# A fused attention and feed-forward kernel: the written-out instruction order of its head is replaced, and the products without a result stand elsewhere

## The chip, the cores and the metric

The kernel runs on one core of a Trainium2 chip. The metric is the device time of one execution in microseconds (us); the time of a version is the median of several runs. Before the change it is 657.39 us, the median of 3 runs (656.91 to 659.03).

## What is computed

```python
# q, k, v: (4 batches, 8 heads, 768 positions, 64); float32
k_sum = k.reshape(B, H, 24, 32, D).max(axis=3)      # a summary key per 32 positions
v_sum = v.reshape(B, H, 24, 32, D).mean(axis=3)     # a summary value per 32 positions
scores_l = scale * q @ k.T          # only |i - j| < 16 is kept, the rest gets -1e9
scores_s = scale * q @ k_sum.T + log(32)
a = softmax(concatenate([scores_l, scores_s]))
attn = a @ concatenate([v, v_sum])
x = attn with heads side by side    # (3072 tokens, 512)
out = ((x @ w_a) * (x @ w_b)) @ w_out               # d_ff = 1536
```

The result has to agree with a float32 computation, so each float32 operand of the large products is split into a high part that TensorE takes in one pass (fp32r) and the rest, a low part.

## The kernel before

**Tiles.** A tile is 128 query positions with all heads. Tokens are worked in chunks: batch 0 in three chunks of two tiles, batches 1 to 3 in chunks of three tiles. For a chunk the attention is computed first, then 12 items of the feed-forward part: item f takes the columns f*128 and on of `w_a` and `w_b` (line 1121: two accumulations h), multiplies the two (DVE), splits the product into gh and gl (ACT, DVE) and multiplies by a row block of `w_out` (line 1243: accumulation into the banks o0 to o3).

**The head.** Until the first item can start, the first four tiles of batch 0 go through a special path, `first_attention`. It has these steps, which the prediction speaks of:

- six loads of keys (line 353, 256 KB each), each turned by four transposes on TensorE (line 503), copied to `kT` by ACT (561, 562), and reduced to block maxima by DVE (569);
- four loads of queries (256 KB each), also turned by line 503 and scaled by ACT (978);
- the mask product (691) and the scores (704), both into the banks o0 to o3; maxima on DVE (737), 32 exponentials a pair of tiles on ACT (751), reciprocals (760, 771) and a diagonal matrix (778) on DVE; a product that turns and normalizes the weights at once (799), its copy by ACT (811);
- the block means of v: six loads ("halves of v", 256 KB each, tiles space10 to space12 of the queue's rows below), an addition of neighbours on POOL (1005), a product with a 0 to 1/32 matrix (996) into bank h0, copies by ACT (1014) and POOL (1020) into the value tiles vw0, vw1 and space12;
- the loads of the value rows of a tile (three loads of 64 to 192 KB), the product of weights and values (852), and its split into x (ACT 881, DVE 885), from which the first item reads.

Beside this, the weights are converted to high and low parts: a load (385, 512 KB) brings half a pair, ACT extracts (420), DVE shifts, masks and multiplies (428, 435, 441), ACT rounds (473), POOL forms the low part (478, 484). Weights are converted in this way until about 150 us.

**What sets the order.** Every operation is recorded with `add` (class `Work`, line 107) and gets a number. `emit` (132) then writes the instructions engine by engine. Without a table it plans with costs in numbers; for the head, `ORDER` (line 24) is a table that for each of the five engines lists the numbers of the operations one after the other. An operation is written only when it is the next one of its engine's list; when a list has run out, the planner goes on by its own rules. SP issues almost all DMAs, also in the order of its list. An engine runs its instructions strictly in the written order, so one that waits holds all behind it.

**Products without a result.** `SPIN` (line 97) lists 16 products of the identity by itself, with the bank that they write and their width (line 1354). Nothing reads them. They are recorded last, as operations 2676 to 2691, and only the list of TensorE says where they stand:

```python
for bk, n in SPIN:
    pe(-1, n / 600, (), (), lambda bk=bk, n=n: nc.tensor.matmul(bank[bk][:, :n], ident, ...))
```

Of the kernel before, what the change touches and what calls it, by code (L numbers as in the profile page):

```python
# [25 lines left out]
        2676 2677 13 2678 5 2679 1 2680 2681 21 2682 17 9 2683 75 57 55 77 58 78 2684-2686 96 98  # L26
        2687-2689 111 100 113 121 102 141 123 104 106 124 143 151 2690 153 154 2691 115 145 173
        171 542 543 180 175 550 178 548 182 549 555 557 556 558 565 563 564 572 570 573 571 582
        583 580 578 581 579 588 590 354 591-593 602 589 600 598 603 599 601 612 610 611 613 608
        609 622 618 623 620 619 621 632 630 628 633 629 631 642 643 640 638 641 639 650 648 510  # L30
        652 673 653 649 651 662 660 658 661 682 659 667 679 687 668 688 940 941 948 946 947 793
        955 953 954 962 960 849 961 967-969 976 974 975 983 903 981 829 982 990 997 988 989 1004
        995 996 883 1002 1003 1046 1009 1011 1018 1010 937 1016 1017 1023 1024
    """,
    "ACT": """
# [8 lines left out]
        806 809 958 802 963 965 970 972 857 977 855 854 862-864 861 865 979 856 689 984 858 986  # L44
        830 991 993 998 915 917 918 916 911 919 910 1000 909 908 1005 912 1007 884 1012 1014
        1019 1021 938 1051 1054 1058 1059 1052 1060 1053 1055 1061
    """,
    "DVE": """
        7 3 15 23 19 11 195 59 60 80 79 196 65 72 66 73 67 74 197 199 85 86 200 87 92 93 201 94
        209-211 213 126 214 223 215 224 125 225 227 138 228 139 156 131 155 132 140 133 168 229  # L50
# [5 lines left out]
        462 625 378 463 627 464 466-468 381 479 374 480 635 481 483 637 484 485 376 496 383 497  # L56
        645 498 500-502 377 373 380 384 513 511 514 647 512 792 698 699 711 527 700 520 712 655
# [1331 lines left out]
```

## Time and profile before

| what | value |
|---|---|
| median of 3 runs | 657.39 us |
| the profiled execution's own time | 657.1 us |
| its span, from the first to the last instruction | 655.3 us |
| TensorE (PE) busy | 644.9 us, 98% |
| VectorE (DVE) | 417.2 us, 64% |
| ScalarE (ACT) | 257.7 us, 39% |
| GpSimd (POOL) | 187.9 us, 29% |

The profiled execution's time is 1.8 us longer than its span, and 0.3 us below the median of the runs. TensorE is busy nearly everywhere, so the page as a whole says only that the kernel is bound by the products; the head is read from the timelines of the single engines, where each row gives the start, the length, what is written from what, and in brackets the idle time of the engine before it and what ended that.

### The profile page before, as it was taken

The page shows a single profiled execution, that of the slowest core. Times are in us where ns is not written, and L with a number is a line of the kernel's source. Part 1 is how long each engine was busy: PE and PEld are TensorE (multiplying, and loading weights), DVE is VectorE, ACT ScalarE, POOL GpSimd, SP SyncE. Part 2 cuts the span into 40 slices and gives each one's busy share as a digit, 9 for nine tenths or more (in the row PEclk, how much of TensorE's full clock was granted, in tenths as well). Part 3 has the DMA queues.
Part 4 walks back from the last instruction along what each step waited for, and adds up shares of the span by engine and source line. Part 5 has one row for each costly group of instructions (what it writes and reads, how often), then busy time and mean ns, then how long its engine had stood idle before and what let it go on. Part 6 is the DMA issues. An engine that isn't in the chain of part 4 may idle for free.

```text
span 655.3 us, 13767 instructions
## 1 busy us (share of the span) xinstructions
PE 644.9 (98%) x5327; PEld 597.1 (91%) x5327; DVE 417.2 (64%) x869; ACT 257.7 (39%) x761; POOL 187.9 (29%) x246
## 2 busy tenths in 40 slices
PE   8899999999999999999999999999999999999997
PEld 6689888899989999999999999999999999999997
DVE  3899999997786776566547478467556557122212
ACT  4997675523434341233414441144324334121111
POOL 6498999847334431011101101011011011000000
PEclk9999999999999999999999999999999999999999
DMA  9999676354443444321112114132111200010001
GB/s 219 279 275 253 230 189 173 73 104 124 124 97 66 121 90 67 62 75 27 37 23 74 33 31 67 26 95 40 28 16 26 74 5 20 1 49 1 0 1 49
DMA packets 158201, 54.76 MB, mean 84 GB/s; under 512 B 135736, under 2 KB 151352, under 8 KB 158136
## 3 DMA queue, kind: packets, MB, share of 16 engines
q1 hardware_dynamic: 157992, 53.75, 34.2%
q8 instruction: 42, 0.69, 0.5%
q14 instruction: 23, 0.19, 0.1%
q10 hardware_dynamic: 144, 0.13, 0.1%
HBM read 47.41 MB, written 6.44 MB: 82 GB/s over the span
## 4 chain that ended last, share of the span: by engine, by line
PE 89%; DMA 5%; SPq 4%; ACT 1%; issue 1%; POOL 0%; DVE 0%; DVEq 0%; ACTq 0%
PE h L1121 54%; PE o L1243 28%; PE c L704 3%; SPq L353 3%; PE o L852 3%; DMA raw<-in_moe_w_a_dram 2%; DMA raw<-in_moe_w_b_dram 2%; SPq L385 1%; PE c L1121 1%; PE h L852 1%; DMA qin<-in_q_dram 1%; POOL space L478 0%; PE c L852 0%; ACT vw L1014 0%; PE o L691 0%
## 5 line engine op out<-in xcount | busy, mean ns | idle before, releaser
L1121 PE MATMUL h<-x,w 128*128 128x384 f32 (+2 forms) x2064 | 388.9, 321 | 0.0
L1121 PEld LDWEIGHTS h<-x,w 128*128 128x128 f32 x2064 | 331.4, 190 | 10.2 <-issue 0.5
L1243 PE MATMUL o<-w,gh 128*128 128x512 f32 x534 | 131.1, 381 | 0.0
L1230 ACT CAST gh<-h 128x384 fp32r<-128x384 f32 x71 | 34.0, 478 | 208.0 <-DVE h L1228 207.4
L1228 DVE TENSOR_TENSOR h<-h,g 128x384 f32<-128x384 f32 x71 | 40.1, 565 | 115.1 <-PE h L1121 109.6
L786 POOL TENSOR_TENSOR s<-s,nml 128x480 f32<-128x480 f32 x40 | 39.4, 987 | 244.6 <-DVE nml L771 243.9
L832 DVE STREAM_TRANSPOSE pt<-s 32x256 f32<-32x256 f32 x228 | 99.4, 436 | 15.1 <-POOL s L786 10.3
L1243 PEld LDWEIGHTS o<-w,gh 128*128 128x128 f32 x534 | 97.9, 189 | 11.2 <-ACT gh L1175 0.5
L1121 PE MATMUL h<-late,w 128*128 128x384 f32 x288 | 93.9, 326 | 0.0
L751 ACT ACTIVATE s<-s,nml 128x120 f32<-128x120 f32 x160 | 61.4, 386 | 17.5 <-DVE nml L737 17.5
L1243 PE MATMUL o<-w,gl 128*128 128x512 f32 x231 | 64.1, 384 | 0.0
L1121 PEld LDWEIGHTS h<-late,w 128*128 128x128 f32 x288 | 54.4, 189 | 0.9
L1225 ACT COPY g<-h 128x384 f32<-128x384 f32 x71 | 34.0, 479 | 51.7 <-PE h L1121 51.5
L1233 DVE TENSOR_TENSOR gl<-h,gh 128x384 fp32r<-128x384 f32 x71 | 39.2, 552 | 21.2 <-ACT gh L1230 20.6
L1243 PEld LDWEIGHTS o<-w,gl 128*128 128x128 f32 x231 | 42.8, 189 | 7.3 <-issue 1.6
L635 POOL TENSOR_TENSOR S<-S 96x256 f32<-96x256 f32 (+3 forms) x58 | 33.0, 571 | 44.6 <-DMA S<-in_v_dram 41.7
L420 ACT ACTIVATE c<-raw 128x512 f32<-128x512 f32 x36 | 29.2, 812 | 12.9 <-DVE S L428 5.6
L751 ACT ACTIVATION_READ_ACCUMULATOR s<-s,nml 128x1 f32 x160 | 30.1, 188 | 0.0
L877 DVE TENSOR_TENSOR o<-o,s 128x512 f32<-128x512 f32 x12 | 8.4, 700 | 32.6 <-ACT s L874 32.5
L478 POOL TENSOR_TENSOR space<-space,w 128x1024 f32<-128x1024 f32 (+1 forms) x14 | 26.7, 1912 | 3.5 <-ACT w L473 3.2
L484 POOL TENSOR_TENSOR w<-space 128x1024 fp32r<-128x1024 f32 (+1 forms) x14 | 26.7, 1911 | 0.9
L729 DVE SCALAR_TENSOR_TENSOR s<-c,mask 128x480 f32<-128x480 f32 x40 | 25.7, 648 | 1.2 <-PE c L704 1.1
(141 smaller groups left out, 645.0 us busy)
## 6 DMA issues: line engine op xcount, KB each, us to landing
raw<-in_moe_w_a_dram SPq DMA_DIRECT2D x12, 512.0 KB, 6.1
raw<-in_moe_w_b_dram SPq DMA_DIRECT2D x12, 512.0 KB, 7.7
raw<-in_moe_w_out_dram SPq DMA_DIRECT2D x12, 512.0 KB, 5.3
out_dram<-S SPq DMA_DIRECT2D x23, 256.0 KB, 2.2
qin<-in_q_dram SPq DMA_DIRECT2D x288, 16.0 KB, 1.8
S<-in_v_dram SPq DMA_DIRECT2D x24, 192.0 KB, 2.8
kin<-in_k_dram SPq DMA_DIRECT2D x38, 100.0 KB, 2.6
vw<-in_v_dram SPq DMA_DIRECT2D x18, 192.0 KB, 3.4
```

Of the source, the lines that this page charges most:

```text
L420: nc.scalar.activation(bank["c0"], high[:, :, 1].bitcast(F32), AF.Prelu, scale=2.0**-112, alpha=-(2.0**32))
L478: lambda ms=ms, f8=f8: nc.gpsimd.tensor_tensor(out=f8, in0=f8, in1=parted(0)[:, ms].bitcast(F32), op=ALU.subtract),
L635: lambda: nc.gpsimd.tensor_tensor(out=out, in0=i0, in1=i1, op=ALU.add),
L751: lambda h=h, c=c, sums=sums: nc.scalar.activation(s[h][:, c, :], x[h][:, c, :], AF.Exp, bias=m[:, 0, h, c : c + 1], scale=1.0, accum_out= ...
L786: lambda h=h, r=r: nc.gpsimd.tensor_tensor(out=s[h], in0=s[h], in1=r[:, :, None].broadcast_to([P, NP, KN]), op=ALU.mult,),
L832: lambda js=js, qs=qs, rs=rs: nc.vector.transpose(out=pv[js, rs, qs], in_=sv[qs, rs, js]),
L1121: nc.tensor.matmul(ps, w[:, c, part, :], (xt[:, 4 * xpart : 4 * xpart + 4] if both else inputs_of(u, xpart))[:, :, c].rearrange("p g (a b) ...
L1225: act(CHAIN, 0.13 + W / 1030, [ak], gk, lambda: nc.scalar.copy(out=g, in_=pa))
L1228: lambda: nc.vector.tensor_tensor(out=pb, in0=pb, in1=g, op=ALU.mult),
L1230: act(CHAIN, 0.16 + W / 1030, [bk], [ghk], lambda: nc.scalar.copy(out=gh, in_=pb))
L1233: lambda: nc.vector.tensor_tensor(out=gl, in0=pb, in1=gh.bitcast(F32), op=ALU.subtract),
L1243: nc.tensor.matmul(bank[ok[j]], (gh if first else gl)[:, j * P : (j + 1) * P], w[:, :, part, :].rearrange("p (z a) n -> p z n a", a=2), st ...
```

## The change

The five lists of `ORDER` are replaced, and the 16 entries of `SPIN` keep their widths but mostly write other banks. No operation is added, taken away or changed. The lists are now a little longer at the end for PE, ACT and DVE, and the one of SP is one entry shorter. The core of the difference is:

```diff
     "PE": """
-        2676 2677 13 2678 5 2679 1 2680 2681 21 2682 17 9 2683 75 57 55 77 58 78 2684-2686 96 98
-        2687-2689 111 100 113 121 102 141 123 104 106 124 143 151 2690 153 154 2691 115 145 173
+        2687 2691 2680 13 1 2683 5 9 17 21 55 2681 57 2682 2677 58 75 2690 77 78 2686 2688 2679
+        2684 111 96 113 121 98 141 123 124 143 151 100 2689 153 154 2678 102 104 106 2676 2685
...
     "SP": """
-        12 4 0 16 20 8 40 39 186 42 43 41 53 187 44 189 46 45 190 192 54 193 49 48 51 47 50 52
+        12 0 4 8 16 20 39 44 186 40 187 42 53 41 189 54 190 192 43 193 46 45 237 48 49 47 52 50
...
 SPIN = [
-    ("h1", 512), ("h1", 128), ("h1", 64), ("h1", 64), ("h1", 256), ("h1", 256), ("h1",
-    128), ("h1", 128), ("h1", 256), ("h1", 256), ("h1", 256), ("h1", 256), ("h1", 256),
-    ("h1", 256), ("h1", 256), ("h1", 128)
+    ("h1", 512), ("o3", 128), ("h1", 64), ("h0", 64), ("o0", 256), ("o0", 256), ("o3", 128),
+    ("o0", 128), ("h0", 256), ("h1", 256), ("h0", 256), ("o0", 256), ("h0", 256), ("h1", 256),
+    ("o3", 256), ("o0", 128),
 ]
```

In the written program the first 718 of 4313 products of TensorE stand in another order (the 718th starts at about 130 us in the profiled execution), and the other 3595 in the same one. On ACT the last 401 of 570 instructions, on DVE the last 656 of 869, on POOL the last 132 of 242 and on SP the last 256 of 538 loads and stores stand as before; in front of these, one load of q on SP comes three places later among its like.

The line numbers of the changed kernel are higher by 4: line 503 of before is 507 there, 1354 is 1358, 691 is 695, 996 is 1000, 852 is 856, 353 is 357 and 385 is 389.

**Place 1: the first instructions of TensorE.** The rows give line, operation, bank written and tiles read, and the shape; `ident` by itself is a product without a result, space8 and space9 hold the loaded keys and queries. Before:

```order
L1354 MATMUL h1_78<-ident_68 128x512
L1354 MATMUL h1_78<-ident_68 128x128
L503 MATMUL o3_76<-ident_68,space8_180 128x128 x4
L1354 MATMUL h1_78<-ident_68 128x64
L503 MATMUL c1_80<-ident_68,space8_180 128x128 x4
L1354 MATMUL h1_78<-ident_68 128x64
L503 MATMUL c0_79<-ident_68,space8_180 128x128 x4
L1354 MATMUL h1_78<-ident_68 128x256 x2
L503 MATMUL c1_80<-ident_68,space9_181 128x128 x4
L1354 MATMUL h1_78<-ident_68 128x128
L503 MATMUL c0_79<-ident_68,space9_181 128x128 x4
```

Now:

```order
L1358 MATMUL o0_73<-ident_68 128x256
L1358 MATMUL o0_73<-ident_68 128x128
L1358 MATMUL o0_73<-ident_68 128x256
L507 MATMUL o3_76<-ident_68,space8_180 128x128 x4
L507 MATMUL c0_79<-ident_68,space8_180 128x128 x4
L1358 MATMUL o0_73<-ident_68 128x128
L507 MATMUL c1_80<-ident_68,space8_180 128x128 x4
L507 MATMUL o2_75<-ident_68,space8_180 128x128 x4
L507 MATMUL c0_79<-ident_68,space9_181 128x128 x4
L507 MATMUL c1_80<-ident_68,space9_181 128x128 x4
L507 MATMUL h0_77<-ident_68,space9_181 128x128 x4
L1358 MATMUL o0_73<-ident_68 128x256
```

640 columns without a result stand ahead of the first turned keys in both; between the following groups of transposes there were such products at nearly every place, and now there is one of 128 columns.

**Place 2: the queue of SP.** The rows are DMA issues: raw are weights, space10 and space11 from in_v the halves of v, space12 and vw the value rows of a tile. Before, from the first load of queries on:

```order
L353 DMA space9_181<-in_q_dram 128x8x64 x2
L385 DMA raw0_205<-in_moe_w_a_dram 128x4x256
L353 DMA space10_182<-in_v_dram 128x4x128 x3
L353 DMA space8_180<-in_q_dram 128x8x64
L385 DMA raw0_205<-in_moe_w_b_dram 128x4x256
L353 DMA space10_182<-in_v_dram 128x4x128
L385 DMA raw1_274<-in_moe_w_out_dram 128x1024
L353 DMA space11_183<-in_v_dram 128x4x128 x2
L385 DMA raw1_274<-in_moe_w_a_dram 128x4x256
L385 DMA raw2_292<-in_moe_w_b_dram 128x4x256
```

Now, from the third load of queries on:

```order
L357 DMA space8_180<-in_q_dram 128x8x64
L357 DMA space10_182<-in_v_dram 128x4x128
L389 DMA raw1_243<-in_moe_w_out_dram 128x1024
L357 DMA space8_180<-in_q_dram 128x8x64
L389 DMA raw1_243<-in_moe_w_a_dram 128x4x256
L389 DMA raw2_260<-in_moe_w_b_dram 128x4x256
L357 DMA space10_182<-in_v_dram 128x4x128
L389 DMA raw2_260<-in_moe_w_out_dram 128x1024
L357 DMA space11_183<-in_v_dram 128x4x128 x2
L389 DMA raw3_281<-in_moe_w_a_dram 128x4x256
L357 DMA vw1_159<-in_v_dram 32x8x64
```

The last halves of v stood behind 6 loads of keys, 3 of queries and 3 of weights; they stand behind 6, 4 and 6. The value rows of the first two tiles stood behind 6 loads of weights and stand behind 7.

**Place 3: TensorE ahead of the first product of weights and values.** h0 from space10 and space11 are the block means, h0 from pt and vw is tile 0's product with the values. Now:

```order
L1358 MATMUL h1_78<-ident_68 128x64
L1000 MATMUL h0_77<-space10_182,space12_184 128x256
L1000 MATMUL h0_77<-space11_183,space12_184 128x256 x2
L1358 MATMUL h1_78<-ident_68 128x512
L1358 MATMUL h1_78<-ident_68 128x256
L856 MATMUL h0_77<-pt_157,vw0_158 64x64 x2
L856 MATMUL h0_77<-pt_157,vw1_159 64x64 x2
```

Before, all six means had been formed ahead of the scores of tile 2, and only one product of 128 columns without a result stood at this place; three of the six have moved behind the scores of tile 3, with 768 columns without a result after them.

## Rows read from the trace of the kernel before

**Rows 1.** The page: busy time of the engines, the granted clock of TensorE in 40 slices of the span, and the chain that ended last by engine.

```profile
PE 644.9 (98%) x5327; PEld 597.1 (91%) x5327; DVE 417.2 (64%) x869; ACT 257.7 (39%) x761; POOL 187.9 (29%) x246
PEclk9999999999999999999999999999999999999999
PE 89%; DMA 5%; SPq 4%; ACT 1%; issue 1%; POOL 0%; DVE 0%; DVEq 0%; ACTq 0%
```

**Rows 2.** The timeline of TensorE, 0 to 130 us, in order of time: start, length, instruction, number of records, idle time before and what ended it.

```profile
1.43 2.50 PE L1354 MATMUL h<-ident 128*128 128x512 f32 x4 [1.43 <-POOL ident masks.py:199]
4.06 1.12 PE L503 MATMUL o<-ident,space 128*128 128x128 f32 x4
...
8.97 0.63 PE L503 MATMUL c<-ident,space 128*128 128x128 f32 x4 [0.99 <-DMA space<-in_k_dram]
...
11.31 0.66 PE L503 MATMUL h<-ident,space 128*128 128x128 f32 x4 [0.34 <-DMA space<-in_q_dram]
11.72 1.13 PE L691 MATMUL o<-space 128*128 128x480 f32 x4
...
14.46 1.05 PE L704 MATMUL o<-kT,qT 64*64 64x120 f32 x32
...
18.51 1.13 PE L996 MATMUL h<-space,space 128*128 128x256 f32 x4 [0.69 <-POOL space L1005]
...
21.44 1.11 PE L799 MATMUL o<-pt,s 128*120 128x128 f32 x8 [0.50 <-ACT space L751]
...
31.96 1.14 PE L691 MATMUL o<-space 128*128 128x480 f32 x4 [1.57 <-ACT space L978]
...
34.44 1.15 PE L852 MATMUL h<-pt,vw 120*64 120x64 f32 x32
35.42 1.10 PE L852 MATMUL h<-space,space 120*64 120x64 f32 x32
36.72 1.98 PE L799 MATMUL o<-pt,s 128*120 128x128 f32 x16 [0.20 <-DVE pt L778]
38.65 2.92 PE L1121 MATMUL h<-x,w 128*128 128x256 f32 x24
...
48.21 1.15 PE L852 MATMUL o<-space,space 120*64 120x64 f32 x32
...
74.20 1.05 PE L704 MATMUL c<-kT,qT 64*64 64x120 f32 x32 [0.16 <-DVE qT L1065]
```

**Rows 3.** Busy time of the products without a result alone (line 1354) in four stretches of the head, with the number of records, the granted clock, the DMA share and GB/s.

```profile
1.40:5.69 4.29, 3.03 (x6) 1.72 (x6) 1.00 1.03 200
5.69:11.30 5.61, 2.13 (x10) 1.59 (x10) 1.00 1.35 219
0.00:38.65 38.65, 9.27 (x32) 6.11 (x32) 1.00 1.07 246
```

**Rows 4.** Busy time of PE, weight loads, DVE, ACT and POOL in stretches of 10 us (instructions in brackets), then granted clock, DMA share and GB/s.

```profile
20.00:30.00 10.00, 9.50 (x90) 8.06 (x89) 9.40 (x22) 8.98 (x26) 2.84 (x5) 1.00 1.16 300
30.00:40.00 10.00, 8.23 (x132) 6.93 (x131) 9.96 (x23) 9.73 (x38) 9.76 (x9) 1.00 0.86 208
40.00:50.00 10.00, 9.92 (x126) 9.16 (x125) 10.00 (x21) 8.84 (x21) 9.05 (x7) 1.00 1.12 309
```

**Rows 5.** The queue of SP in its timeline: start of the first issue, length, tile and number of issues.

```profile
16.94 2.09 SPq L353 DMA_DIRECT2D space<-in_v_dram  x2
19.08 0.63 SPq L385 DMA_DIRECT2D raw<-in_moe_w_a_dram  x1
...
27.61 3.41 SPq L353 DMA_DIRECT2D space<-in_v_dram  x2
```

**Rows 6.** DMA issues of 0 to 36 us: number, size of each, median us from issue to landing.

```profile
space<-in_v_dram SPq DMA_DIRECT2D x1, 192.0 KB, 5.9
```

**Rows 7.** The same columns as rows 4, in shorter stretches.

```profile
16.00:20.00 4.00, 3.31 (x28) 2.49 (x18) 2.80 (x5) 3.46 (x21) 2.09 (x3) 1.00 1.15 311
20.00:24.00 4.00, 3.50 (x26) 3.02 (x25) 3.82 (x12) 3.04 (x14) 1.09 (x2) 1.00 1.10 330
24.00:28.00 4.00, 4.00 (x45) 3.21 (x47) 3.58 (x8) 3.98 (x10) 1.11 (x2) 1.00 1.13 322
32.00:34.00 2.00, 2.00 (x36) 1.46 (x36) 2.00 (x6) 2.00 (x10) 2.00 (x2) 1.00 0.94 226
```

**Rows 8.** The way of the block means behind the last half of v in the timeline of POOL.

```profile
24.53 0.73 POOL L1005 TENSOR_TENSOR space<-space 128x256 f32<-128x256 f32 x1 [0.15 <-DMA space<-in_v_dram]
...
31.29 0.60 POOL L1020 COPY space<-vw 24x512 f32<-24x512 f32 x1
```

**Rows 9.** The copies of the block means and the split of the first two products with the values in the timeline of ACT.

```profile
27.97 1.17 ACT L1014 COPY vw<-h 24x512 f32<-24x512 f32 x2
...
36.66 1.08 ACT L881 CAST x<-h 128x512 fp32r<-128x512 f32 x2
```

**Rows 10.** The transposes (line 503) before 5.5 us and after 6.4 us: duration in ns, least, median and greatest, first and last start.

```profile
L503 PE MATMUL o<-ident,space x4: 421/421/476, 4.1 to 4.8; 128*128 128x128 f32 x4
L503 PE MATMUL c<-ident,space x12: 272/273/328, 6.5 to 10.0; 128*128 128x128 f32 x12
```

More of the change, by code (lines that the diff above doesn't have):

```diff
@@ L25 @@
     "PE": """
-        2676 2677 13 2678 5 2679 1 2680 2681 21 2682 17 9 2683 75 57 55 77 58 78 2684-2686 96 98
-        2687-2689 111 100 113 121 102 141 123 104 106 124 143 151 2690 153 154 2691 115 145 173
-        171 542 543 180 175 550 178 548 182 549 555 557 556 558 565 563 564 572 570 573 571 582
-        583 580 578 581 579 588 590 354 591-593 602 589 600 598 603 599 601 612 610 611 613 608
-        609 622 618 623 620 619 621 632 630 628 633 629 631 642 643 640 638 641 639 650 648 510
@@ L31 @@
-        652 673 653 649 651 662 660 658 661 682 659 667 679 687 668 688 940 941 948 946 947 793
-        955 953 954 962 960 849 961 967-969 976 974 975 983 903 981 829 982 990 997 988 989 1004
-        995 996 883 1002 1003 1046 1009 1011 1018 1010 937 1016 1017 1023 1024
[6 rows of a table added]
+        948 946 947 793 955 953 954 962 960 849 961 967-969 976 974 975 983 903 981 829 982 990
+        997 988 989 1004 995 996 883 1002 1003 1046 1009 1011 1018 1010 937 1016 1017 1023 1024
+        1080 1081 1088 1086 1087 1089 1096 1094 1095 1121 1122 1097 1160 1102 1103 1161 1168
@@ L34 @@
+        1166 1167 1169
     """,
     "ACT": """
[8 rows of a table removed]
[8 rows of a table added]
         806 809 958 802 963 965 970 972 857 977 855 854 862-864 861 865 979 856 689 984 858 986
         830 991 993 998 915 917 918 916 911 919 910 1000 909 908 1005 912 1007 884 1012 1014
-        1019 1021 938 1051 1054 1058 1059 1052 1060 1053 1055 1061
+        1019 1021 938 1051 1054 1058 1059 1052 1060 1053 1055 1061 1082 1025 1062 1084 1090 1092
+        1098 1123 1125 1131-1133 1100 1134 1162 1135 1138-1142 1164 1170
     """,
     "DVE": """
-        7 3 15 23 19 11 195 59 60 80 79 196 65 72 66 73 67 74 197 199 85 86 200 87 92 93 201 94
@@ L50 @@
-        209-211 213 126 214 223 215 224 125 225 227 138 228 139 156 131 155 132 140 133 168 229
[5 rows of a table removed]
-        462 625 378 463 627 464 466-468 381 479 374 480 635 481 483 637 484 485 376 496 383 497
-        645 498 500-502 377 373 380 384 513 511 514 647 512 792 698 699 711 527 700 520 712 655
-        713 701 657 702 533 703 531 536 532 534 704 539 705 538 664 540 535 530 537 737 541 684
-        666 714 738 686 715 675 739 716 681 717 724 718 725-729 671 730 943 731 740-742 945 743
[5 rows of a table removed]
+        3 7 15 19 11 23 195 59 60 196 197 65-67 79 72 73 80 74 199 85 86 200 87 201 92 209 93
[6 rows of a table added]
@@ new lines @@
+        384 464 625 380 377 466 627 467 376 468 382 479 480 381 635 373 481 637 483-485 378 379
+        496 497 645 498 500-502 374 383 375 513 514 511 698 647 699 512 700 711 712 701 527 702
+        713 655 520 792 657 533 703 531 536 532 534 704 539 705 538 664 540 535 530 537 737 541
+        684 666 714 738 686 715 675 739 716 681 717 724 718 725-729 671 730 943 731 740-742 945
[4 rows of a table added]
+        1120 1049 939 1022 1050 1056 1027 1083 1063 1085 1068-1076 1091 1077 1078 1093 1079 1124
+        1127 1128 1126 1099 1129 1130 1101 1200 1136 1143 1163 1148 1149 1165 1150-1158
@@ L65 @@
     """,
     "POOL": """
-        36-38 26 32 35 29 99 97 95 101 105 103 108 203 110 206 204 207 217 220 221 231 232 218
-        234 235 248 249 262 263 276 277 290 291 304 305 334 335 348 349 372 397 398 365 411 412
-        425 426 439 440 453 454 456 457 470 471 473 474 487 488 490 491 529 504 505 507 508 528
-        521 748-751 754-759 1293 706 732 719 1294 1295 745 763-765 1297 766 1298-1300 811 804
+        36-38 32 26 29 35 95 101 97 206 99 203 207 105 103 217 110 108 204 220 221 218 231 232
@@ L71 @@
+        234 235 248 249 262 263 276 277 290 291 304 334 335 305 348 349 397 398 411 412 425 426
+        439 365 372 453 454 456 457 440 470 471 473 474 487 488 490 491 529 504 505 507 528 521
+        508 748-751 754-759 1293 706 732 719 1294 1295 745 763-765 1297 766 1298-1300 811 804
         769-772 1302 773 774 1303-1305 1307-1310 867 860 1314-1316 1311 1318-1321 921 914
```

52 rows, old and new, of the table ORDER are left out of this document.

## The prediction

> **What bounds the kernel now.** I read the page first. TensorE is busy for 644.9 of 655.3 us and PE holds 89% of the chain that ended last [rows 1], so the end is set by the products: it comes when TensorE has done its fixed work, plus whatever time it stood idle or ran products that nobody reads. All of it that the page leaves is 655.3 - 644.9 = 10.4 us. Next, the timeline of TensorE shows where that lies: gaps of 1.43, 0.99, 0.34, 0.69, 0.50, 1.57 and 0.20 us stand ahead of 38.65 us, and the next row with a gap above the pipeline's own is one of 0.16 us at 74.20 [rows 2]. The first feed-forward item starts at 38.65 us. From there on there is a queue of finished work in front of TensorE, and a change of the order pays or costs only what it moves that start, or what it breaks in the queue behind it. Third, the products without a result: 9.27 us of TensorE's time before 38.65 us [rows 3]. They lie where it would wait anyway, so they are idle time by another name. Idle and idle-like time of the head is thus some 15 us, and the question is what the head itself waits for.
>
> Fourth, the stretches of 10 us answer that. Between 20 and 40 us DVE is busy for 9.40 and 9.96 of 10 us, ACT for 8.98 and 9.73, while TensorE stands at 9.50 and 8.23 with the products without a result in it, and the DMA share is 1.16 and 0.86 [rows 4]. So two engines and the wire are full at once: the order can hardly make this stretch shorter, it can only choose who waits. That is the reader's first lesson from these rows: the 15 us are not there to be taken.
>
> **The change part by part.** No operation is added or removed, so the sum has only moved waits. I follow the chain to the first item.
>
> *Keys, queries, first scores.* The loads of keys pace the first 11 us in both. Before, the first scores start at 14.46 us [rows 2], behind two turned tiles of queries and both mask products. Now tile 0 needs one tile of queries: from its landing at 11.31 us [rows 2] come its transposes, 256 columns without a result, one mask product and 2 x 128 columns, about 2.6 us, so the scores start near 13.8. This gains up to 0.6 us for ACT and DVE at that point. Since both are full afterwards, and the values come later anyway, I count nothing for it on the path. The cover that hides the gain is the wire; without it, the 0.6 us would be a gain.
>
> *Block means.* The last half of v is issued at about 18.5 us (second of the two issues from 16.94) [rows 5] and is added on POOL at 24.53, right after landing [rows 8]. Now 3 loads of weights (512 KB) and one of queries (256 KB) more stand ahead of it: 1.84 MB. The wire moves 311 to 330 GB/s in this stretch [rows 7], so that is 1.84 MB / 0.32 MB per us = 5.7 us: landing near 30.1 and 30.8 once added (0.73). The last product of the means (0.6 us) ends by 31.4 if TensorE is free, two copies on ACT (1.17) [rows 9] by 32.6, and POOL's copies for tile 1 (2 x 0.60) [rows 8] by 33.9. Before, this chain ended at 31.29 + 0.60 = 31.9 with 2.5 us to spare against the product at 34.44; now it has 0.5 us to spare for tile 1's. Its copies stand in ACT's queue, which is full, so up to one instruction in front (0.6 us) may push it. I take zero, and keep +0.6 for the range.
>
> *Value rows.* Before, the last issue for tile 1 goes out at 28.3 us, and its like (192 KB) lands 5.9 us after issue [rows 5, 6]: 34.2 us. TensorE reached tile 1's product at 35.42 [rows 2], so 1.2 us were to spare. Now one 512 KB load of weights more stands ahead: 0.524 MB / 0.32 = 1.6 us, hence 35.8. The spare 1.2 us are used up and **0.4 us are late**. Nothing better is queued at that place: behind the waiting product stand tile 2's turns (line 799) and the first item, and ACT's split of x (1.08 us) [rows 9], which it feeds. Part of this returns, because before TensorE waited 0.20 us for the diagonal at 36.72 [rows 2], which will by then be there: +0.4 - 0.1 = **+0.3 us** for the first item, 38.65 to about 38.95. Ends: -0.2 if the wire is no later than before, +1.0 if the rows land at the pace of 226 GB/s shown for 32 to 34 us [rows 7] (0.524 / 0.226 = 2.3 us, of which 1.2 are spare).
>
> *SP's next loads.* Before and now the loads of tile 2's value rows wait, at the head of SP's queue, for tile 0's product, since they write the same buffer; the weights behind them wait as well. Tile 0's product at 34.44 keeps its place within 0.3 us, so I count nothing beyond the +0.3.
>
> *Behind the first item.* Tile 3's product with the values stood at 48.21 us, 9.56 us behind the first item [rows 2]; now it stands right behind the second item and both of the turns, one item's `w_out` products and so about 1 us earlier. Its value rows and ACT's copy have 1 us less. I take **+0.2 us** (ends 0 and +0.6). The weights' conversion is reordered up to about 150 us, but between 42 and 74 us TensorE has no idle row, so a shift of some tenths there is covered. If that cover were gone, the price is the row at 74.20: 0.16 us a place.
>
> *Products without a result.* Columns are the same, so their time is the same unless the clock changes (below). Writing h0, o0 and o3 instead of h1, they now wait for the readers of these banks; they stand where TensorE waits anyway: 0.
>
> The sum is +0.3 + 0.2 = **+0.5 us**. Against the profiled execution's own 657.1 us (span 655.3 and 1.8 around it) that gives 657.6; this execution lies 0.3 us below the median of the runs, 657.39, so for a median I say **657.9 us**. A measurement of this kernel can tell about 0.3% (2.0 us) from no change, so my forecast is no change that can be told.
>
> **The rivals.** *The clock comes up late* (ends slower). Until about 5.5 us a group of four transposes takes 421 ns a piece, from 6.5 on 272 [rows 10]; the piece from 4.06 lasts 1.12 us, later ones 0.63 to 0.66 [rows 2]. So TensorE begins at the lower level (1.2 GHz) and had 4.13 of 4.29 us of activity, 3.03 of them products without a result, when it rose; between 5.69 and 11.30 another 2.13 us of these followed [rows 3]. Now 640 columns run at the start, and until 11.3 us nearly only transposes, some 0.45 us in every 1.2 at the full rate. If the clock rises only when the real products start, the first tile's turn, mask product and scores (0.66 + 1.13 + 1.05 and the 512 columns between them, some 3.2 us at 2.4 GHz) take up to 6.4. They feed ACT and DVE directly, and those have no slack behind: up to +3.2 us, +1.6 if it rises halfway. With the +0.5: 659.0 to 661.1 us. It decides once it rises later than about 14 us. For it: nearly every product between the keys is gone. Against: the transposes at half rate fill 0.9 of each 1.2 us, and the clock stayed up through the idle 0.99 and 1.57 us of before [rows 1, 2]. The Trainium skill, "TensorE: Matmul & The Clock Gate", section "Part 4: PE-mode transpose", says that transposes do not count as busy for the clock in the way that products do; by that rule the clock would come late here, and this rival would win. The rows of before cannot decide it, since there products stand between all transposes while the clock rises. Chance 0.3, of which two thirds lie over the line of 2.0 us, 659.4.
>
> *The head gets shorter* (faster). If the wire does not bind and tile 3's queries, which now come two loads earlier, take away the wait of 1.57 us at 31.96, and with it the 0.50 and 0.20 [rows 2], the first item starts up to 2.3 us earlier: 657.4 - 2.3 = 655.1 us. For it: this is the longest wait late in the head. Against: the value rows cannot land before 34 us, and tile 0's product stood at 34.44, so most of the gain meets the wire. Chance 0.1.
>
> *The means become the bound* (slower, but little). If the wire is a tenth slower than its rows, 5.7 us become 6.3 and the values' 1.6 become 1.8; with ACT's 0.6 on top the first item is 1.5 us late: 658.9 us, by itself inside what cannot be told. Chance 0.15, of which 0.04 over the line, with a wire slower still.
>
> *The tables do nothing*: the orders printed differ in all engines, so this is excluded; what is the same is everything behind 130 us.
>
> **How the numbers follow.** The forecast itself has 0.45. No change 0.67: that, 0.11 of the late means, 0.10 of the late clock and 0.01 of the shorter head. Slower 0.24: 0.20 of the clock and 0.04 of the means. Faster 0.09: the shorter head where it reaches its full price. The range holds 8 in 10: below, the sum with a gain of 1.8 us, 656.0; above, the late clock without its last microsecond, 660.2.
>
> **What would show it.** Right: the first item (line 1125 in the new numbering) starts between 38.5 and 39.5 us; the last half of v is added on POOL near 30; tile 1's product waits for the value rows until about 35.8; behind 40 us TensorE's gaps are tenths; the tail is the same. The late clock would show as transposes of 421 ns after 6.5 us and scores of 2 us; the shorter head as a first item before 37 us. I am wrong if the first item starts outside 37 to 41 us, or if TensorE loses more than 1 us between 40 and 130 us, where I count 0.2.

## The result, and the profile after

| | us |
|---|---|
| before, median | 657.39 (656.87 to 659.03, 7 runs) |
| changed, median | 661.45 (659.55 to 662.98, 7 runs) |
| ratio | 1.0062, interval 1.0051 to 1.0073 |
| changed, profiled execution: time and span | 659.55 and 657.8 |

The change is 0.6% slower (4.06 us in the medians), clear of what the measurement can tell, and outside the range given. The profiled execution is the quickest of its seven runs and the only one with a mean granted clock of 0.999; the others have 0.994 to 0.997. So its trace can show 2.5 us (span 657.8 against 655.3), and the further 1.9 us of the median must be sought in what the other runs have and it has not.

The page of the changed kernel [rows 1] tells nothing of this. TensorE is busy for 2.1 us more with the same work, since a product that takes longer also counts as busy: the transposes of the head (line 503) make up 0.9 us of it, the products of weights and values (852) 0.5.

```profile
PE 647.0 (98%) x5327; PEld 598.2 (91%) x5327; DVE 418.5 (64%) x869; ACT 257.3 (39%) x761; POOL 187.9 (29%) x246
```

The timeline of TensorE after the change, which answers to [rows 2]:

```profile
5.51 1.11 PE L507 MATMUL c<-ident,space 128*128 128x128 f32 x4
6.42 0.63 PE L1358 MATMUL o<-ident 128*128 128x128 f32 x2
6.84 0.99 PE L507 MATMUL c<-ident,space 128*128 128x128 f32 x4
7.91 0.66 PE L507 MATMUL o<-ident,space 128*128 128x128 f32 x4
...
13.95 1.05 PE L708 MATMUL o<-kT,qT 64*64 64x120 f32 x32
...
34.81 1.15 PE L856 MATMUL h<-pt,vw 120*64 120x64 f32 x32 [0.36 <-ACT vw L1018]
35.79 1.10 PE L856 MATMUL h<-space,space 120*64 120x64 f32 x32
...
39.16 2.92 PE L1125 MATMUL h<-x,w 128*128 128x256 f32 x24 [0.29 <-ACT space L755]
...
48.80 0.30 PE L856 MATMUL o<-space,space 120*64 120x64 f32 x2 [0.89 <-DMA space<-in_v_dram]
49.70 1.15 PE L856 MATMUL o<-space,space 120*64 120x64 f32 x30 [0.60 <-ACT space L815]
```

The first item starts 0.51 us later than before. The rest, 1.95 of 2.46 us, is lost behind it, and 1.49 us of that stand in the last two rows: tile 3's product with the values, which had no wait before, now waits for its value rows and then for ACT's copy of the turned weights. At 130 us TensorE is 2.31 us behind the kernel before, and from 140 us to the end it is 2.46, so nearly all is decided by 130.

What ACT did meanwhile, in the kernel before (line 420 extracts a loaded weight, 811 copies tile 3's turn, 1200 makes gh). Here raw4 and raw5 are the buffers of weights that the loads of 37.87 and 40.65 us fill, or those of 38.28 and 38.88 us after the change:

```profile
43.46 0.38 ACT L1200 CAST gh<-h 128x256 fp32r<-128x256 f32 x1
43.72 0.60 ACT L881 CAST x<-o 128x512 fp32r<-128x512 f32 x1
44.20 0.61 ACT L811 COPY space<-o 120x512 f32<-120x512 f32 x1
44.99 0.76 ACT L420 ACTIVATE c<-raw 128x512 f32<-128x512 f32 x1 [0.18 <-DVE space L428]
...
47.45 0.59 ACT L811 COPY space<-o 120x512 f32<-120x512 f32 x1 [0.47 <-PE o L799]
47.94 0.38 ACT L1200 CAST x<-h 128x256 fp32r<-128x256 f32 x1
48.20 0.69 ACT L420 ACTIVATE c<-raw 128x512 f32<-128x512 f32 x1
```

And after the change (424 extracts, 815 copies, 1204 makes gh):

```profile
44.19 0.65 ACT L424 ACTIVATE c<-raw 128x512 f32<-128x512 f32 x1 [1.15 <-DMA raw<-in_moe_w_a_dram]
44.77 0.58 ACT L815 COPY space<-o 120x512 f32<-120x512 f32 x1
45.25 0.58 ACT L885 CAST x<-o 128x512 fp32r<-128x512 f32 x1
47.17 0.76 ACT L424 ACTIVATE c<-raw 128x512 f32<-128x512 f32 x1 [1.34 <-DVE c L439]
47.86 1.03 ACT L477 CAST w<-S 128x1024 fp32r<-128x1024 f32 x1
48.80 0.37 ACT L1204 CAST gh<-h 128x256 fp32r<-128x256 f32 x1
49.06 0.59 ACT L815 COPY space<-o 120x512 f32<-120x512 f32 x1
```

Before, the extractions of raw4 and raw5 (44.99, 48.20) stand each behind a copy and a cast of h, and their loads have landed when ACT gets there (43.9 and 47.8 us by the DMA records). After, ACT stands idle for 1.15 us until raw4 lands (44.1). The 1.34 us at 47.17 are put down to a DVE step, but raw5 lands at 47.09, so it is the load that ends it. gh and tile 3's copy are queued behind. The loads are not late (raw4 lands within 0.2 us of before, raw5 0.7 us earlier): the engines come to them too early, with finished work behind them. DVE shows the same: it was busy for 10.00 of 10 us from 40 to 50 us [rows 4], and is now for 8.52 (columns as in rows 4):

```profile
40.00:50.00 10.00, 8.51 (x101) 7.97 (x101) 8.52 (x17) 7.43 (x16) 7.13 (x6) 1.00 1.10 264
```

SP in the kernel before:

```profile
38.40 2.19 SPq L353 DMA_DIRECT2D space<-in_v_dram  x3
40.65 1.42 SPq L385 DMA_DIRECT2D raw<-in_moe_w_b_dram  x1
```

And after the change:

```profile
36.03 0.31 SPq L357 DMA_DIRECT2D vw<-in_v_dram  x1
...
38.28 0.55 SPq L389 DMA_DIRECT2D raw<-in_moe_w_a_dram  x1
38.88 0.82 SPq L389 DMA_DIRECT2D raw<-in_moe_w_b_dram  x1
39.80 2.90 SPq L357 DMA_DIRECT2D space<-in_v_dram  x3
```

Tile 3's three loads of value rows (the last row) go out behind raw4 and raw5; before, raw5 came after them. By the DMA records they land at 47.5, 48.7 and 49.4 us instead of 45.6, 46.2 and 46.5. The second ends the wait of 0.89 us; the third lies within the next wait, of 0.60, which ACT's copy ends at 49.65.

### The profile page after: what moved, and what is told of

It is laid out like the page before. It is cut to its first block, busy times and chain, and to the rows that moved or that the text cites. A ratio compares the mean times of both kernels' runs of the same rounds, so it can differ in the third digit from the quotient of the medians.

```text
span 657.8 us, 13763 instructions
## 1 busy us (share of the span) xinstructions
PE 647.0 (98%) x5327; PEld 598.2 (91%) x5327; DVE 418.5 (64%) x869; ACT 257.3 (39%) x761; POOL 187.9 (29%) x246
## 4 chain that ended last, share of the span: by engine, by line
PE 86%; SPq 4%; DMA 3%; POOL 2%; issue 2%; DVE 1%; ACT 1%; DVEq 0%; POOLq 0%; ACTq 0%
PE h L1125 52%; PE o L1247 27%; SPq L357 3%; PE o L856 3%; PE c L708 3%; DMA raw<-in_moe_w_a_dram 2%; POOL w L488 1%; SPq L389 1%; POOL space L482 1%; DMA raw<-in_moe_w_b_dram 1%; PE c L1125 1%; PE h L856 1%; ACT c L424 1%; DVE c L439 0%; PE c L856 0%
```

## The experiments

All were timed in 5 rounds beside the kernel before, which was 656.93 to 657.07 us in these measurements, with a mean granted clock of 0.999 or 1.0 in each of its 70 runs. The ratio is formed over all runs, with its 95% interval, and is not the quotient of the medians. "Behind" is the later end of the span, less the later start of the first item, both against the kernel before, from the profiles; a profile is one run and need not be the median one (that of e6_early_before is the quickest of its five, that of e11_warm_line the second of eleven).

| kernel | median | ratio to before | first item | behind |
|---|---|---|---|---|
| e1_again | 660.19 | 1.0054 [1.0042, 1.0067] | 39.64 | +2.1 |
| e12_again | 659.40 | 1.0042 [1.0029, 1.0054] | 38.90 | +2.0 |
| e2_warm | 659.62 | 1.0043 [1.0030, 1.0055] | 38.90 | +2.4 |
| e3_bare | 657.60 | 1.0008 [0.9998, 1.0017] | 38.74 | +0.4 |
| e4_queues | 660.78 | 1.0060 [1.0047, 1.0072] | 39.59 | +2.3 |
| e5_early_after | 657.93 | 1.0010 [1.0002, 1.0019] | 39.11 | +0.3 |
| e6_early_before | 660.29 | 1.0046 [1.0033, 1.0059] | 38.43 | +2.4 |
| e7_adp | 666.93 | 1.0153 [1.0130, 1.0176] | 38.44 | +9.4 |
| e8_warm_late_before | 657.26 | 1.0002 [0.9993, 1.0011] | 38.41 | +0.3 |
| e9_line_ad | 659.81 | 1.0037 [1.0025, 1.0050] | 38.93 | +2.4 |
| e10_line_ads | 659.17 | 1.0029 [1.0019, 1.0039] | 39.63 | +1.2 |
| e11_warm_line | 659.22 | 1.0027 [1.0019, 1.0036] | 38.84 | +1.2 |
| e13_warm_copy | 657.49 | 1.0005 [0.9996, 1.0014] | 38.45 | +0.6 |

### The change again, twice

e1_again and e12_again are the changed kernel itself.

> The changed kernel once more, unchanged, for more clocks beside more times, and a second profile. If the waits behind the first item (1.49 us at tile 3's product with the values, 0.51 at the first item) are the same in each execution and the rest is the clock, this profile shows the same waits to within 0.3 us, and its time goes with its mean granted clock: about 659.6 us at 0.999, 661.5 at 0.997, 663 at 0.994. If the scatter lies in the waits, the waits differ between the two profiles and the clock does not.

> The changed kernel a third time. In the first measurement its median was 661.45 us with mean granted clocks of 0.994 to 0.997 in the runs above 661, in the second 660.19 with 0.996 to 1.0. If the clock can fall a second time, in the waits behind the first item (TensorE is busy for 0.60 of 2 us from 48 to 50), a run with a mean clock of 0.994 shows a granted clock under 1 between 46 and 52 us as well as before 16 us, and its time is 661.5 us or more. If only the fall before 16 us exists, its price is 0.7 us and the times stay between 659.5 and 660.7.

The waits are there again, 1.60 us at tile 3's product in e1_again, 1.59 in e12_again with 0.40 of it at tile 2's: they are in every profile of the change. The granted clock is not, and its link with the time is looser than expected: 659.9 and 660.2 us at 1.0, 660.2 to 661.9 at 0.996. The profile of e1_again, windows of the head (columns as in rows 4):

```profile
11.00:13.00 2.00, 1.62 (x7) 1.45 (x8) 1.39 (x3) 1.24 (x3) 0.73 (x4) 0.69 1.13 324
13.00:15.00 2.00, 2.00 (x8) 1.72 (x7) 0.13 (x1) 0.63 (x1) 0.51 (x3) 0.50 1.21 278
15.00:17.00 2.00, 2.00 (x40) 1.70 (x39) 1.15 (x3) 0.00 (x0) 0.00 (x0) 0.96 1.18 306
```

The transposes show when the clock came up: they take 421 ns at first and 272 or 273 from about 5 us on, but for the first of a group (the column of the granted clock does not tell it: it reads 1.00 before the first rise too [rows 3, 10]). At about 11.8 us the clock fell again to the lower level, 1.2 GHz, after six groups of transposes with hardly a product between, and it stayed there through the first tile's mask product and scores, to about 15.2 us. In e12_again, with the same instructions, it came up only at 9.4 us, then held at 1.00, and the first item started 0.74 us earlier:

```profile
39.64 2.92 PE L1125 MATMUL h<-x,w 128*128 128x256 f32 x24 [0.15 <-ACT space L755]
```

```profile
13.00:15.00 2.00, 1.73 (x38) 1.35 (x36) 0.13 (x1) 0.63 (x1) 0.58 (x3) 1.00 1.20 279
38.90 2.92 PE L1125 MATMUL h<-x,w 128*128 128x256 f32 x24 [0.29 <-ACT space L755]
```

The first fence is e1_again, the second e12_again. So the fall cost **0.74 us** at the first item. Each profile with a fall has a mean clock of 0.996 or 0.997, each without one 0.999 or 1.0, so I count a run of 0.997 or less as one with a fall. Over all 17 runs of the change, 11 had one and a median of 661.2 us; the 6 others had 659.5. That is 1.7 us (2.1, 0.6 and 1.6 in the three measurements by themselves), more than the 0.74 of the profile. The fall of e1_again, half the clock for 3.4 of 658.4 us, takes 0.0026 from its mean of 0.996; a second one like it would bring the mean to 0.994, that of the two runs of 662 to 663 us, so these may have had two. This is an estimate from one profile: none shows a second fall in the change, and e12_again, from which I expected one, has no run under 0.996. Its times, 659.2 to 661.2 us, also spread further than the 659.5 to 660.7 expected for a single fall.

### The clock alone

e2_warm puts five products without a result back between the first transposes of the change:

```diff
-        2687 2691 2680 13 1 2683 5 9 17 21 55 2681 57 2682 2677 58 75 2690 77 78 2686 2688 2679
+        2687 2691 2680 13 2692 1 2683 5 2693 9 2694 17 2695 21 2696 55 2681 57 2682 2677 58 75 ...
-    ("o3", 256), ("o0", 128),
+    ("o3", 256), ("o0", 128), ("h1", 64), ("h1", 256), ("h1", 256), ("h1", 256), ("h1", 256),
```

> The changed kernel with five more products without a result (64 and 4 x 256 columns, 1088 in all) between the first groups of transposes, about where the kernel before had such. Nothing else moves. Theory 'clock' (without them the clock comes up late, or falls again after it came up): the granted clock is at full speed from about 5.7 us on, the mean is 0.999 in every run, and the median falls by 1.5 to 2.5 us, to about 659.3. Theory 'queues' alone (all of the loss is in waits behind reordered loads and copies): the time stays at 661.4 within 0.5, or rises by up to 0.5 us.

The same windows of e2_warm:

```profile
11.00:13.00 2.00, 2.00 (x12) 1.46 (x11) 1.37 (x3) 1.24 (x3) 0.75 (x4) 1.00 1.13 324
13.00:15.00 2.00, 1.79 (x38) 1.41 (x36) 0.00 (x0) 0.60 (x1) 0.48 (x2) 1.00 1.21 279
```

The clock holds once it is up (at about 8 us here, in the three profiles of the change at 5.0 to 9.4), and it does so in all 38 runs of the four kernels with these five products (e2_warm, e8, e11, e13). The first item is where e12_again has it. But the median is 659.62, 0.57 under e1_again's, which was measured beside it: the clock is a part of the loss, and with it held 2.5 us remain. The 1.5 to 2.5 us of the theory were counted from the 661.45 of the first measurement, from which it is 1.8; beside e1_again they were too much. The other theory's "stays or rises" failed too.

e3_bare takes the products between the transposes out of the kernel before:

```diff
-        2676 2677 13 2678 5 2679 1 2680 2681 21 2682 17 9 2683 75 57 55 77 58 78 2684-2686 96 98
-        2687-2689 111 100 113 121 102 141 123 104 106 124 143 151 2690 153 154 2691 115 145 173
+        2676 2677 13 5 2678 2679 1 21 17 9 75 57 55 77 58 78 2684-2686 96 98
+        2687-2689 111 100 113 121 102 141 123 104 106 124 143 151 2690 2680-2683 153 154 2691 ...
```

> The kernel before, with the products without a result that stood between the first groups of transposes (640 columns) moved behind the head's last mask products; the two at the very start (640 columns) stay. Nothing else moves. Theory 'clock': it takes over the late clock of the change and its scatter, 658.5 to 660 us, with mean granted clocks of 0.994 to 0.998 instead of 0.999. Theory 'queues' alone: 657.4 within 0.5.

Its profile has the fall as well, only earlier:

```profile
7.50:9.00 1.50, 0.00 (x0) 0.00 (x0) 1.02 (x2) 1.00 (x4) 1.16 (x8) 0.81 1.36 218
9.00:11.00 2.00, 1.90 (x9) 1.93 (x10) 0.36 (x2) 0.65 (x2) 1.73 (x7) 0.50 1.35 218
11.00:13.00 2.00, 2.00 (x13) 1.78 (x11) 1.68 (x3) 1.72 (x5) 0.19 (x1) 0.79 1.17 285
```

But only 2 of its 11 runs had a fall, where the kernel before had none in 70, and these two (657.57 and 656.97 us) are not slower than the nine others (median 657.63). So the 0.5 us of the median, whose ratio takes in no change, are not the fall's, and the time is the one that the theory of the queues gave. In the profile the first item comes 0.09 us later: the clock is back at about 11.8 us, before the scores. By these profiles the price of a fall goes by where it lies: nearly none over the transposes, 0.7 us over the first scores. That products between the transposes hold the clock rests on both sides together, none of 108 runs with them and 2 of 11 or 11 of 17 without, and not on this run alone.

### Two repairs in the queues

e4_queues moves tile 3's value rows ahead of raw5's load on SP, and tile 3's copy and gh ahead of raw5's extraction on ACT:

```diff
-ACT ... 179 176 267 247 546 181 551
+ACT ... 179 176 181 546 267 247 551
-SP  ... 252 265 149 148 150 266
+SP  ... 252 149 148 150 265 266
```

> The changed kernel with two repairs of order: on SP tile 3's three loads of value rows stand ahead of one 512 KB load of weights as before, and on ACT tile 3's copy of the turned weights and item 0's gh stand ahead of the extraction of raw5 as before. Theory 'queues': the two waits of 0.89 and 0.60 us at tile 3's product go, and the time falls by 1 to 1.5 us, to 660 to 660.4; the clocks stay scattered. If these two waits only move to later places (raw5 is then loaded 1.6 us later), the time stays at 661.4 within 0.4.

TensorE in e4_queues behind the second item:

```profile
48.14 1.15 PE L856 MATMUL o<-space,space 120*64 120x64 f32 x32
50.97 1.10 PE L1247 MATMUL o<-w,gh 128*128 128x512 f32 x4 [1.68 <-DVE x L889]
```

Both waits at tile 3's product are gone, and one of 1.68 us stands two rows on, at the split of the same tile on DVE. It was not the loads' place alone: DVE's list too has tile 3's split behind the shift of raw5, and raw5 now lands later. The time, 660.78, is not under that of the change measured beside it (660.19 us). The second branch of the expectation is what happened, the waits only moved; its number (661.0 to 661.8) was counted from the first measurement and is missed.

### Cut at the first item

The lists of both kernels are cut at the first item; one half of each is put together. There is no short diff: the entries up to 171 (TensorE), 146 (ACT), 147 (DVE), 232 (POOL) and 238 (SP) of the lists of before make the front, sorted as in one kernel; the rest follows as in the other. On TensorE and SP the change itself has nothing from behind the cut ahead of it; on ACT, DVE and POOL it has some entries there, and these halves leave that out.

> The lists are cut at the first item (by the kernel before: 48 entries of TensorE, 56 of ACT, 54 of DVE, 24 of POOL, 30 of SP). What stands ahead of the cut is in the order of the change, with its products without a result; what stands behind is in the order of the kernel before. Theory 'behind the first item' (two thirds of the loss is in the order of loads and conversions that serve 40 to 55 us): the waits at tile 3's product with the values go, the time falls from 660.2 to about 657.9 (657.07, plus 0.3 for a later first item, plus 0.5 for the clock). Theory 'front' (the loss is made ahead of the first item, by the clock and the late values, and is only seen later): 659.5 to 660.5, as the change.

> The other half: ahead of the same cut the order and the products of the kernel before, behind it the order of the change. Theory 'behind the first item': the first item starts at 38.65 us as before, TensorE then waits 1.5 to 2 us between 40 and 55 us, time about 659. Theory 'front': 657.1 within 0.4.

> The order of the change ahead of the cut, with the five products of e2_warm, and the order of the kernel before behind it. If the clock and the order behind the first item are the whole loss: 657.3 to 657.7, mean granted clock 0.999 in each run. If something else in the front part costs: 658 or more. Faster than 657.07 only if the first scores, which start 0.5 us earlier in the change, count after all.

TensorE in e5_early_after, and then in e6_early_before:

```profile
39.11 2.92 PE L1125 MATMUL h<-x,w 128*128 128x256 f32 x24
...
43.24 1.15 PE L856 MATMUL o<-pt,vw 120*64 120x64 f32 x32 [0.33 <-ACT pt L815]
...
48.93 1.15 PE L856 MATMUL o<-space,space 120*64 120x64 f32 x32
```

```profile
42.41 1.10 PE L803 MATMUL o<-space,space 128*120 128x128 f32 x8 [1.06 <-ACT c L424]
...
49.41 1.15 PE L856 MATMUL o<-space,space 120*64 120x64 f32 x30 [0.45 <-ACT space L815]
```

This settles in which part of the lists the loss is. The front of the change with the rest of before is +0.95 us, as expected; the front of before with the rest of the change is +3.3 us, as much as the whole change or more, and 1.3 us over the 659 expected. (The two do not add to the change's +2.5 to +3.1, so what the rest costs depends on the front before it.) With the clock held as well (e8), the front of the change costs +0.28, which the interval does not tell from nothing.

Best compared are runs in which the clock held on both sides. With the order of the change behind the cut these have 659.5 us (the 6 runs of the change) and 659.62 (e2), with the order of before 657.42 (6 runs of e5) and 657.26 (e8). So **the order behind the first item costs 2.1 to 2.4 us**. The front itself costs 0.3 to 0.4 against the 657.0 of before, and the fall of the clock 0.7 more (in e5, 658.09 for the five runs with it against 657.42) up to the 1.7 of the change. e6's wait of 1.06 us is put down to an extraction on ACT (424), again one ahead of work that TensorE needs.

e7_adp takes only ACT's, DVE's and POOL's lists behind the cut from the kernel before:

> The change, with only the lists of ACT, DVE and POOL behind the cut taken from the kernel before; TensorE and SP keep the order of the change. If the loss is that finished inputs stand behind the conversion of a load that has not landed (raw5) in the queues of ACT and DVE, whatever the order of the loads: 1.2 to 1.9 us are regained, 658.3 to 659.0. If it is the place of tile 3's value rows on SP: the wait of 0.9 us for these stays, and at most 0.8 is regained, 659.4 to 660.

```profile
43.91 1.10 PE L803 MATMUL o<-space,space 128*120 128x128 f32 x8 [2.55 <-ACT gh L1204]
```

```profile
40.00:50.00 10.00, 7.45 (x74) 7.05 (x73) 6.26 (x13) 5.64 (x15) 6.24 (x5) 0.83 1.13 267
```

```profile
80.21 1.05 PE L708 MATMUL c<-kT,qT 64*64 64x120 f32 x32 [3.02 <-DVE qT L1069]
60.00:130.00 70.00, 66.37 (x334) 56.86 (x333) 63.44 (x104) 43.91 (x74) 59.80 (x32) 1.00 0.56 156
```

Neither branch held: +9.9 us. Lists of before that meet TensorE's and SP's lists of the change are worse than either whole; ACT and DVE stand behind products that TensorE makes in another order, and TensorE waits for 2.55 and 3.02 us at two places. The second fence (stretch of 10 us, columns as in rows 4) shows that the clock falls here behind the wait of 2.55 us, to 0.83 over the stretch; behind the longer wait of 3.02 us, in the third fence, it does not fall. The run says that the lists belong together, and nothing on which engine's list is at fault.

### Finished work ahead of loads that have not landed

e9_line_ad stays in the change's lists and alters the two places on ACT and DVE that the profile pointed to; e10_line_ads adds SP's, e11_warm_line the five products:

```diff
-ACT ... 233 257 179 176 267 247 546 181 551 271 183 261
+ACT ... 233 179 257 176 181 546 267 247 551 183 271 261
-DVE ... 258 256 545 259 268 177 260 547 269 272 184 552 270
+DVE ... 258 256 545 259 177 260 547 268 269 184 272 552 270
 (e10, e11)
-SP  ... 252 265 149 148 150 266
+SP  ... 252 149 148 150 265 266
```

(257 and 267 are the extractions of raw4 and raw5, 268 and 269 DVE's steps on raw5; 176 to 184 and 546 belong to tiles 2 and 3 and item 0; 265 is raw5's load.)

> The change, with the lists of ACT and DVE altered at one place each: the extractions of raw4 and raw5 and the shift of raw5 go behind the copies, casts and splits of tiles 2 and 3 and item 0's gh, which do not need these loads. SP and TensorE stay as in the change. Theory 'finished work behind a load that has not landed': of the 1.5 us of waits at tile 3's product the 0.6 behind ACT's copy goes, and the 0.9 for the value rows stays unless POOL or DVE let SP go on earlier: 659.3 to 659.8 beside 660.2 of the change. If the loss is the later landing of the loads themselves, nothing is regained: 660.2 within 0.4.

> The same with tile 3's value rows ahead of one 512 KB load of weights on SP, as in e4_queues. e4 had the two moves on SP and ACT without DVE's, and then TensorE waited 1.68 us for DVE's split of tile 3, which stood behind the shift of raw5. Theory 'finished work behind a load that has not landed': now both waits go, and that of 1.68 shrinks under 0.6: 658.2 to 659.0. If raw5, which is loaded 1.6 us later, is itself what the next items lack: 660 to 660.8, with a wait of TensorE for converted weights between 50 and 60 us.

> e10_line_ads with the five products of e2_warm. If the clock and the order in these three queues are separate and add: 0.5 to 0.7 below e10_line_ads, 657.6 to 658.5, with mean granted clocks of 0.999 and 1.0. The kernel before is 657.0.

In e9 the wait of 0.6 us for ACT's copy went and that for the value rows grew to 1.88. Its clock held in all five runs, so its 659.81 us stand against the 659.5 of the change with the clock held: nothing is regained. In e10 both waits are gone, and no wait of their size stands in their place:

```profile
45.59 2.92 PE L1125 MATMUL h<-x,w 128*128 128x256 f32 x24
48.45 1.15 PE L856 MATMUL o<-space,space 120*64 120x64 f32 x32
49.53 1.13 PE L1247 MATMUL o<-w,gh 128*128 128x512 f32 x4
```

"Behind" falls from 2.0 or 2.1 us to 1.2 in this profile, and the median is +2.1 us, against +2.5 and +3.1 of the change. The expectation of 658.2 to 659.0 was just missed. But the change's medians have more runs with a fall in them (11 of 17) than e10's (1 of 9). With the clock held, e10 has 659.3 us against 659.5, and e11, with the five products, 659.22 against the 659.62 of e2: **the entries moved give back 0.2 to 0.4 us, of the 2.1 to 2.4 that the order behind the first item costs.** The two waits of 1.49 us at tile 3's product are thus where the loss is seen in the change's profile; taking them away returns little of it, so most of the loss hangs on other entries of the order, or comes back in smaller pieces. ACT still comes to the two loads early in e10:

```profile
45.28 0.66 ACT L424 ACTIVATE c<-raw 128x512 f32<-128x512 f32 x1 [1.24 <-DMA raw<-in_moe_w_a_dram]
...
48.70 0.66 ACT L424 ACTIVATE c<-raw 128x512 f32<-128x512 f32 x1 [0.63 <-DMA raw<-in_moe_w_b_dram]
```

The 1.2 us that stay in e10's profile are in no wait of over 0.2 us that the timeline names. Between the first item and the product of weights and values at 126.3 us before, 128.3 in e10, the times from start to start, summed by line, are longer by 0.34 us at h, 0.33 at `w_out`, 0.16 at the turns, 0.15 at the scores and 0.07 at the values, mostly in steps of 0.1 to 0.3. What ends them, and which entries cause them, stays open. e11 has the first item at 38.84 and the clock held, but its median is that of e10, above the 657.6 to 658.5 expected: in its profile another 0.66 us is lost at tile 2's product, and the clock's and the queues' gains did not add.

### The front's gain

In e8 the first item started 0.24 us earlier than before and 0.28 was lost at 42.49 in a wait for a copy on ACT. e13_warm_copy moves that copy:

```diff
-ACT ... 157 174 158 544 172 233
+ACT ... 157 174 172 158 544 233
```

> e8_warm_late_before with one instruction moved: ACT's copy of tile 2's turned weights goes ahead of the last exponential of tile 3 and item 0's copy of h. In e8 the first item started at 38.41 us, 0.24 earlier than in the kernel before, and 0.28 was lost at 42.49 in a wait for this copy, 0.1 more at 74. If that wait was the loss, the time is 656.8 to 657.1, at or just under the kernel before (657.0); if the gain of 0.24 has to be given back at the next engine that is full, 657.2 to 657.4.

The wait is gone, and the time is 657.49, not under the kernel before (ratio 1.0005, no change). The first item starts 0.20 us earlier, and 0.6 us is lost behind it, of which the timeline names one wait, of 0.21 us at 74.59. None of the kernels beats the kernel before.

## Why the prediction was wrong

- *Bound, and the two full engines between 20 and 40 us.* Right, and no order here was faster than before, which fits it but does not prove it. What I did not draw from it is that DVE stays full to 50 us **by a backlog** of loaded weights: with its 10.00 of 10 us from 40 to 50 [rows 4], raw4 and raw5 had landed before they were reached, and I looked for cover on TensorE only.
- *First scores*: 13.8 forecast, 13.95 measured; nothing gained at the end. Right.
- *Block means*: the last half of v landed at 30.5 us (forecast 30.1), but POOL was in a step on weights and added the last two halves from 30.55 to 31.97 (forecast 30.8). The last means stood behind tile 3's mask product and scores and ended at 33.15 (forecast 31.4), ACT's copies at 34.76 (forecast 32.6). Tile 0's product waits 0.36 us for these. That this lies between my 0 and +0.6 is partly luck: the chain was 2.2 us later than its sum, and spare time took up the most of it.
- *Value rows*: forecast to land at 35.8 and to make the first item 0.3 late. They landed at 35.4 and tile 1's product did not wait. The first item was 0.51 late, or 0.25 in e12_again: 0.36 or 0.18 are the wait for the means, and 0.29 at the item itself are put down to ACT's exponentials. The size was about right, the reason was not.
- *SP's next loads*: the wait for tile 0's product ends at 36.03 instead of 35.63. Right.
- **Behind the first item: +0.2 forecast (ends 0 and +0.6), 1.95 measured, 2.1 to 2.4 by the exchange of the order.** This is the step that failed, and by my own sign (more than 1 us lost between 40 and 130 us) it did. I named tile 3's product, its value rows and ACT's copy, and said that these "have 1 us less"; I did not follow the two queues to there. On SP a 512 KB load is put ahead of the value rows (landing 2.9 us later), on ACT and DVE the conversions of raw4 and raw5 ahead of the copies, casts and splits that TensorE waits for. The exchange (e5 and e8 against the change and e2) shows that the loss lies in the order behind the first item. e10 shows that moving just these entries back takes the two waits away, but only 0.2 to 0.4 us of the time: which entries cost the rest stays open. Behind the first item I counted queued work only behind SP's waits, not behind ACT's and DVE's.
- *The price if the cover were gone*, "0.16 us a place": it was 0.89 + 0.60 us at one product.
- *The clock* was a rival at 0.3, and its mechanism is real: 11 of 17 runs had it. It took another form. I looked for a clock that rises late; in the three profiles of the change it rose between 5.0 and 9.4 us, latest where it then held, and in the one with a fall it was down from 11.8 to 15.2. The price at the first item, 0.74 us, is less than the 1.6 to 3.2 that I put on it. (The times of this rival are 659.5 to 661.1 us by my own sum; the 659.0 leaves out the +0.5.) My argument against (it stayed up through idle times of 0.99 and 1.57 us) compared one wait between products with a stretch of nothing but transposes. The Trainium skill, "TensorE: Matmul & The Clock Gate", section "Part 4: PE-mode transpose", says that transposes do not count as busy in the way products do. The rows of e1_again against e2_warm agree, yet 6 of 17 runs of the change kept the clock with the same transposes, and in e12_again it came up in the fifth group of transposes, with a single short product among them. Where page and rows differ, the rows decide.
- The sum: of +2.5 us in the profiled execution 0.5 is the first item and 2.0 the rest. The median's further 1.9 us go with the clock by the runs, of which a profile shows 0.74; where the rest of them is lost stays open.

## What to carry to other kernels

When a hand-written order moves loads, follow every strictly ordered queue to the first instruction that needs the load, and list what stands behind it there: a converter that reaches a load before it has landed holds finished work that the busiest engine needs. A backlog in front of a helper engine can be cover: here DVE and ACT were busier from 20 to 30 us after the change (9.96 and 9.67 of 10 us, 9.40 and 8.98 before [rows 4]) and idle before the loads of 44 and 47 us. And a wait that is seen is not yet what it costs: take it away and time again, with the clock in the same state on both sides, before it is called the cause. Products that nobody reads may hold the clock: see what lies between them when they are moved, and look at the clock of several runs, since one profile may show the run in which it held.

## What the runs showed of the chip

The granted clock of the same program differed from run to run: full from 9.4 us on through the head in e12_again, 0.50 from 13 to 15 us in e1_again. With five products without a result between the early transposes it did not fall in any of 38 runs; without them it fell in 11 of 17 runs of the change and in 13 of 35 of the other kernels with its front (in e7_adp, which has four of these, perhaps at its later wait). A longer wait of TensorE was not by itself what decided it: in one execution of e7_adp the clock fell, to 0.83 over 10 us, behind a wait of 2.55 us and stayed at 1.00 behind one of 3.02, and the 1.57 us of the kernel before [rows 2] and the 1.88 of e9_line_ad left it at 1.00 too.
